# Using the first units' order of work in every unit of a kernel that interleaves a recurrence with a mixture of experts

## The chip, the cores and the metric

One core of one Trainium2 chip. The metric is the device time of one execution in microseconds (us), lower is better. Each run also gives the span of its profile and the mean clock that was granted to TensorE (1 is full). All profiles shown here, and all runs of the variants, were in the fast state. The kernel before varies more (1272 to 1299 us in one set of rounds), and three or four of its runs are marked slow; ratios and gains below use its fast runs alone.

Engines: PE is TensorE's matmuls, PEld its weight loads, DVE VectorE, ACT ScalarE, POOL GpSimd, SP SyncE (here a queue of DMAs). L374 is line 374 of the kernel; in variants with a helper added, lines shift by some ten.

## The reference

Two blocks, one feeding the other. The first is a recurrence over 768 steps for 4 batches of 8 heads with a 40 x 40 state each. The second sends its 3072 x 320 output through four experts (320 to 1024 to 320) and sums them with normalised weights. All is fp32.

```python
for t in range(S):                                   # S = 768
    y[:, :, t] = np.einsum('bhd,bhde->bhe', rt, state)
    Sa = np.einsum('bhde,bhe->bhd', state, at)
    state_decay = state * wt[:, :, None, :] - np.einsum('bhd,bhe->bhde', Sa, bt)
    state = state_decay + np.einsum('bhd,bhe->bhde', vt, kt)
...
for e in range(E):                                   # E = 4
    h = np.maximum(x @ w1[e], 0.0)
    out += p[:, e:e + 1] * (h @ w2[e])
```

## The kernel before

The sequence is cut into 12 chunks of 64 steps, and the batches into two pairs: 24 *units*. For each unit there are three generators of recurrence work, and a list `todo` of mixture pieces (an up-projection `ph`, or half of a down-projection: `p431`, or `p75` and `p26`):

- `within(q)`: work that needs no state. Inputs are transposed on DVE; then come the causal scores `pc` (of V and R) and `pfe`.
- `merge(q)`: three stages, Q's transposes (`Qc`, `QTc`), then `pY`, then `pQ`.
- `step(q)`: `prn`, then `psat`, then `pxr`, `pdy` (the new state and the output Y), then the DMAs from Y into `xT`, the mixture's input.

The parts of `within` that matter: R is the last input to be transposed, and `pc` needs it.

```python
def turn_rv():
    VT = by_channels("VT", "turned", 3, "V")         # a transpose on DVE
    q.RT = by_channels("RT", "RT", 2, "R")           # the next one
    return VT
# ...
NT = by_channels("NT", "turned", 3, "B", rG[:])
q.AT = by_channels("AT", "AT", 2, "A", Gv)
KT = by_channels("KT", "turned", 3, "K", rG[:])
# ...
VT = turn_rv()
yield
pc = quadrants(banks("pc"), 0, BY_TOKENS, L, lambda j, s, i: (
    s, i, j, of_slots(VT, s, j, i, D), of_slots(q.RT, s, j, i, D),
))
```

The mixture's additions run on DVE too: five of `add_h` per expert (`a<-hs`), and eight updates of the output (`osb`). Mixture pieces are taken by `mix`, which after each piece also puts some of the input transfers that are due onto the queue. **How many depends on how many pieces the call takes**:

```python
def begin_later(n):
    for move in later[:n]:
        tc.keep_in_program_order(move(nc.sync))
    del later[:n]

def mix(n):
    for piece in todo[:n]:
        piece()
        begin_later(3 if n > 1 else 6)
    del todo[:n]
```

The loop over units has four gaps for mixture pieces, and two orders of recurrence work around them. The framework's scheduler then orders each engine's instructions; it may move independent ones past each other.

```python
early = u < 5
run(s, 1); run(w, 1); run(s)
# ...
begin_later(len(later))
run(w, 1)                       # rG
if not early: run(m, 1)         # Qc, QTc
gap(1)
# ... the next unit's transfers are listed in `later`
run(w, 1)                       # transposes of B, A, K, V, R
if early: run(m, 1)
else:     run(s_next, 1); run(m, 1)      # prn; pY
gap(2)
if not early: run(m, 1)         # pQ
run(w, 1)                       # pc, pfe
if not early: run(s_next, 1)    # psat
# ...
if early:
    run(m, 1); run(s_next, 1); run(m)    # pY; prn; pQ
    gap(3, 1)                            # one piece
    run(s_next, 1)                       # psat
    mix(0 if 4 * u + 3 in sparse else 1) # one more piece
else:
    gap(3)                               # two pieces at once
```

(The excerpt is shortened, and its comments are mine.)

Of the kernel before, what the change touches and what calls it, by code (L numbers as in the profile page):

```python
# [15 lines left out]
def kernel(  # L16
# [161 lines left out]
    def begin(u):  # L178
        q = Unit()
        q.u, q.c, q.bp = u, u // (B // 2), u % (B // 2)  # L180
        q.b = [2 * q.bp, 2 * q.bp + 1]
        q.start, q.end = q.c == 0, q.c == NC - 1
        q.n = {}
        units.append(q)
        return q

    def load(q, names):
        for x in names:
            q.n[x] = t = sb.tile([P, H, D], FP32, name=f"nat{x}", tag=f"nat{x}", bufs=2 if x == "V" else 1)
            for i, bb in enumerate(q.b):  # L190
                nc.sync.dma_start(
                    out=t[i * L:(i + 1) * L], in_=srcs[x][bb, :, q.c * L:(q.c + 1) * L, :].rearrange("h t e -> t h e"),
                )

    def load_raw(q, names):


        moves = []
        for x in names:
            q.n["raw" + x] = t = raw[x]()  # L200
            heads = srcs[x].rearrange("b h t e -> (b h) t e")[q.b[0] * H:(q.b[1] + 1) * H, q.c * L:(q.c + 1) * L, :]
            heads = heads.rearrange("n (x two) e -> x n (two e)", two=2)
            for r in range(2):
                hs = slice(r, 16, 2)
                for y, los, w_ in ((0, (0,), D + Q), (1, (0, D) if x == "W" else (0,), D - Q if x == "W" else 2 * D - Q)):
                    o = slice(64 * r + Q * y, 64 * r + Q * y + Q)
                    for lo in los:
                        cols = slice(Q * y + lo, Q * y + lo + w_)
                        moves.append(
                            lambda eng, out=t[o, :, lo:lo + w_], in_=heads[:, hs, cols]: eng.dma_start(out=out, in_=in_)  # L210
                        )
        return moves
# [10 lines left out]
    def go(moves, eng=None):  # L223
        for move in moves:
            move(eng or nc.sync)
# [347 lines left out]
    def merge(q):  # L573


        Qc = sb.tile([P, H, Q], FP32, name="Qc", tag="q", bufs=2)
        QTc = sb.tile([P, H, Q], FP32, name="QTc", tag="q", bufs=2)
        tc.keep_in_program_order(nc.vector.transpose(out=dealt(Qc[:]), in_=q.Z))
        tc.keep_in_program_order(
            nc.vector.transpose(  # L580
                out=QTc[:].rearrange("p h r -> p (h r)"), in_=Qc[:].rearrange("p h c -> p (h c)"),
            )
        )
        q.QT = QTs()
        for i in range(P // Q):
            ins = nc.gpsimd.tensor_copy(out=q.QT[quarter(i), :, quarter(i % 2)], in_=QTc[quarter(i)])  # L586
            tc.keep_in_program_order(ins)
        yield

        py = big("pY")  # L590
        for h in range(H):
            for i in (1, 3):
                nc.tensor.matmul(
                    out=py[quarter(i - 1), h * Q:(h + 1) * Q], lhsT=q.F[quarter(i), h, 0:Q],
                    rhs=QTc[quarter(i), h, :], start=True, stop=True,
                )
        Y = sb.tile([P, H, Q], FP32, name="Yq")
        for i in (0, 2):
            nc.scalar.copy(out=Y[quarter(i)].rearrange("p h t -> p (h t)"), in_=py[quarter(i), 0:H * Q])
        yield  # L600

        pq = big("pQ")
        for h in range(H):
            for i in (0, 2):
                nc.tensor.matmul(  # L605
                    out=pq[quarter(i), h * Q:(h + 1) * Q], lhsT=Qc[quarter(i), h, :],
                    rhs=Y[quarter(i), h, :], start=True, stop=True,
                )
        for i in (0, 2):
            nc.scalar.copy(out=q.QT[quarter(i), :, quarter(1)], in_=by(pq[quarter(i), 0:H * Q], Q))  # L610
        yield
# [157 lines left out]
    def mixture_of_unit(q):  # L769

        hs, at = {}, 2 * E * q.u

        def ups(e):
            hs[e] = [up(at + 2 * e + x, q.xT, P, P) for x in range(2)]
            used(at + 2 * e + 2)
            if q.u == 0 and e + 2 < E:
                load_w2(e + 2)

        def down(e):
            po = ps.tile([P, DM], FP32, name="po", tag="mm", bufs=3)  # L780
            for f in range(NF):
                nc.tensor.matmul(  # L782
                    out=po[:], lhsT=hs[e][f // HF][:, f % HF, 0:P], rhs=w2_sb[e][:, f, :],
                    start=(f == 0), stop=(f == NF - 1),
                )
            if e == 0:
                q.osb = outputs()
            add(q.osb[:], po[:], scale(q, e), e == 0)
            if e == E - 1:
                store(q, q.osb)  # L790

        todo.append(lambda: ups(0))
        for e in range(E):
            todo.append(lambda e=e: down(e))
            if e + 1 < E:
                todo.append(lambda e=e: ups(e + 1))
# [113 lines left out]
# [12 lines that stand above are left out]
    def run(gen, n=99):  # L922
        if gen is None:
            return
        for _ in range(n):
            if next(gen, gen) is gen:
                break
# [3 lines left out]
    def begin_step(u):  # L931
        q = units[u]
        if q.bp == 0:
            chunks_x[q.c] = sb.tile([P, 3, 2 * P], FP32, name="xT", tag="xT", bufs=2)
        q.xT = chunks_x[q.c][:, :, q.bp * P:(q.bp + 1) * P]
        return step(q, q.xT)
# [79 lines left out]
    for u in range(1, NU):  # L1016
        q = units[u]
        m = s_next = w = w_next = iter(())
        if u + 1 < NU:
            m, s_next = merge(units[u + 1]), begin_step(u + 1)  # L1020
            w_next = ws[u + 1]
        if u + 2 < NU:
            w = ws[u + 2]

        def gap(n, pieces=None):
            at = 4 * u + n
            run(sum_ops, sums_at.get(at, 0))
            mix((1 if at in sparse else 2) if pieces is None else pieces)

        run(w, 1)  # L1030
        run(w_next)
        run(s, 1)
        gap(0)


        early = u < 5
        run(s, 1)
        run(w, 1)
        run(s)
        if u == 1:  # L1040
            mixture_of_unit(q)
        elif q.bp:
            mixture_of_chunk(units[u - 1:u + 1], chunks_x[q.c])
        begin_later(len(later))
        run(w, 1)
        if not early:
            run(m, 1)
        gap(1)

        if u + 3 < NU:  # L1050
            go(load_raw(begin(u + 3), "W"))
            load(units[u + 3], "BKV")
            later.extend(load_raw(units[u + 3], "BAKVR"))
        run(w, 1)
        if early:
            run(m, 1)
        else:
            run(s_next, 1)
            run(m, 1)
        gap(2)  # L1060

        if not early:
            run(m, 1)
        run(w, 1)
        if not early:
            run(s_next, 1)
        if u + 2 < NU:
            substitute(units[u + 2], nc.gpsimd)
        run(w, 1)
        if u + 3 < NU:  # L1070
            ws.append(within(units[u + 3]))
            run(ws[u + 3], 1)
        if early:
            run(m, 1)
            run(s_next, 1)
            run(m)
            gap(3, 1)
            run(s_next, 1)
            mix(0 if 4 * u + 3 in sparse else 1)
        else:  # L1080
            gap(3)
        s = s_next
# [31 lines left out]
```

## Time and profile before

| | before |
|---|---|
| time, median of 2 fast runs | 1282.74 us (1276.39 to 1289.1) |
| span of the profile, mean granted clock | 1283.8 us, 0.887 |
| the last 16 units but one | 832.8 us, 52.05 us each |
| of these: PE busy, PE idle | 795.45 us, 37.35 us |
| half clock in them | 211.6 us |
| PE's waits for RT in them | 16 of 2.16 us |

The "16 units" are counted from the first `pdy` matmul of one unit to that of the sixteenth unit after it; the same stretch is cut from every trace below. It is the steady part: the start and the tail are not touched by the argument. The table's third and fourth rows come from the view of busy time in a stretch. Its columns are: the stretch, its length, busy us of PE (with the number of instructions), PEld, DVE, ACT and POOL, PE's granted clock, the DMA engines' mean busy share, GB/s.

```profile
312.70:1145.50 832.80, 795.45 (x10529) 696.01 (x10528) 546.04 (x1063) 218.40 (x556) 337.70 (x863) 0.87 0.40 94
```

Idle time is the length less PE's busy time, 37.35 us. A busy PE at clock 0.87 is not a PE at work at full speed: a matmul at half clock counts as busy for longer (16 dense ones took 6.13 us there and 3.72 us at full clock, as the prediction shows). So this line has two kinds of loss in it, idle time and slow busy time, and the count (10529 matmuls) makes the second visible when another kernel does the same matmuls in less busy time.

One more view of before is needed later, the DMA queue's own timeline (start, duration, queue, line, transfer, count):

```profile
629.78 0.97 SPq L210 DMA_DIRECT2D rawR<-in_r_dram  x2
630.85 9.31 SPq L718 DMA_DIRECT2D xT<-Y  x12
640.21 0.97 SPq L210 DMA_DIRECT2D rawR<-in_r_dram  x2
```

Half of R stands behind xT's twelve transfers, and is issued at 640.2 to 641.2 us.

### The profile page before, as it was taken

The page shows a single profiled execution, that of the slowest core. Times are in us where ns is not written, and L with a number is a line of the kernel's source. Part 1 is how long each engine was busy: PE and PEld are TensorE (multiplying, and loading weights), DVE is VectorE, ACT ScalarE, POOL GpSimd, SP SyncE. Part 2 cuts the span into 40 slices and gives each one's busy share as a digit, 9 for nine tenths or more (in the row PEclk, how much of TensorE's full clock was granted, in tenths as well). Part 3 has the DMA queues.
Part 4 walks back from the last instruction along what each step waited for, and adds up shares of the span by engine and source line. Part 5 has one row for each costly group of instructions (what it writes and reads, how often), then busy time and mean ns, then how long its engine had stood idle before and what let it go on. Part 6 is the DMA issues. An engine that isn't in the chain of part 4 may idle for free.

```text
span 1283.8 us, 38036 instructions
## 1 busy us (share of the span) xinstructions
PE 1200.6 (94%) x15828; PEld 1045.6 (81%) x15828; DVE 829.7 (65%) x1642; ACT 331.1 (26%) x844; POOL 475.2 (37%) x1226
## 2 busy tenths in 40 slices
PE   5889988999999999999989999999999999999998
PEld 4767766888788888888878888888888887888887
DVE  7865576789656756676566666676666766644334
ACT  2222333223223122232231322322213323122110
POOL 4024555464253351552524515425244253350000
PEclk7789987999797887997979899789797997899999
DMA  7657642445334424443343443442434334212221
GB/s 147 141 135 196 137 91 67 98 101 125 84 99 100 105 74 99 95 114 85 84 109 85 108 104 87 104 99 72 107 86 112 86 104 89 84 57 86 86 76 31
DMA packets 299491, 126.73 MB, mean 99 GB/s; under 512 B 244360, under 2 KB 272696, under 8 KB 299320
## 3 DMA queue, kind: packets, MB, share of 16 engines
q1 hardware_dynamic: 296312, 123.84, 40.5%
q8 instruction: 125, 2.05, 0.7%
q10 hardware_dynamic: 3008, 0.46, 0.2%
q14 instruction: 46, 0.38, 0.1%
HBM read 116.36 MB, written 3.93 MB: 94 GB/s over the span
## 4 chain that ended last, share of the span: by engine, by line
PE 75%; DVE 10%; SPq 7%; DMA 5%; issue 2%; ACT 1%; DVEq 0%; ACTq 0%
PE ph L741 25%; PE p L848 20%; PE ph L733 9%; SPq L718 3%; PE pfe L374 3%; PE pdy L374 2%; PE psat L374 2%; PE prn L374 2%; DMA w1p<-in_moe_w_dram 2%; PE po L782 2%; SPq L210 2%; PE pxr L374 2%; PE pQ L605 2%; DVE osb L759 2%; PE pc L374 1%
## 5 line engine op out<-in xcount | busy, mean ns | idle before, releaser
L741 PE MATMUL ph<-xT,w1p 128*128 128x256 f32 (+1 forms) x1520 | 370.1, 400 | 0.0
L741 PEld LDWEIGHTS ph<-xT,w1p 128*128 128x128 f32 x1520 | 293.3, 203 | 74.6 <-issue 26.3
L567 POOL TENSOR_TENSOR Z<-Z 128x31 f32<-128x31 f32 (+7 forms) x704 | 256.9, 365 | 55.2
L554 POOL TENSOR_TENSOR Z<-M,Z 128x62 f32<-128x62 f32 (+7 forms) x352 | 156.0, 443 | 294.9 <-DVE M L545 258.6
L842 DVE TENSOR_TENSOR a<-hs 128x512 f32<-128x512 f32 x220 | 152.5, 710 | 145.6 <-ACT hs L746 145.6
L746 ACT ACTIVATE hs<-ph 128x512 f32<-128x512 f32 (+1 forms) x208 | 117.2, 564 | 439.9 <-PE ph L741 439.6
L759 DVE SCALAR_TENSOR_TENSOR osb<-p,gate,osb 128x320 f32<-128x320 f32 (+1 forms) x243 | 108.1, 480 | 128.6 <-PE p L848 125.1
L848 PE MATMUL p<-sums,a 128*128 128x160 f32 x1056 | 164.8, 299 | 0.0
L586 POOL COPY QT<-QTc 32x256 f32<-32x256 f32 x96 | 40.1, 418 | 326.7 <-DVE QTc L580 309.1
L848 PEld LDWEIGHTS p<-sums,a 128*128 128x128 f32 x1056 | 152.9, 190 | 2.2
L733 PE MATMUL ph<-xT,w1p 64*128 64x256 f32 (+1 forms) x760 | 138.1, 442 | 0.6 <-ACT xT L710 0.6
L848 PE MATMUL p<-w,hs 128*128 128x160 f32 x704 | 104.2, 301 | 0.0
L848 PE MATMUL p<-w,a 128*128 128x160 f32 x704 | 102.8, 299 | 0.0
L848 PEld LDWEIGHTS p<-w,hs 128*128 128x128 f32 x704 | 100.8, 191 | 2.3
L848 PEld LDWEIGHTS p<-w,a 128*128 128x128 f32 x704 | 98.0, 190 | 0.0
L733 PEld LDWEIGHTS ph<-xT,w1p 64*128 64x128 f32 x760 | 79.5, 207 | 20.1 <-issue 6.3
L439 DVE RECIPROCAL rG<-G 128x504 f32<-128x504 f32 x24 | 79.1, 3296 | 0.0
L634 ACT COPY SN<-prn 64x256 f32<-64x256 f32 x88 | 32.2, 366 | 159.0 <-DVE EV L630 156.6
L529 DVE STREAM_TRANSPOSE M<-blocks 128x1024 f32<-128x1024 f32 x24 | 46.3, 1931 | 35.4 <-ACT blocks L526 35.1
L374 PE MATMUL pc<-RT,VT 40*64 40x64 f32 x768 | 21.2, 264 | 40.4 <-DVE RT L229 39.0
L374 PEld LDWEIGHTS pc<-RT,VT 40*64 40x64 f32 x768 | 17.3, 168 | 46.7 <-DVE RT L229 43.6
L374 PE MATMUL pdy<-VC,k_tok 64*64 64x104 f32 (+1 forms) x768 | 43.6, 269 | 0.0
(153 smaller groups left out, 1489.7 us busy)
## 6 DMA issues: line engine op xcount, KB each, us to landing
w1p<-in_moe_w_dram SPq DMA_DIRECT2D x95, 512.0 KB
w1p<-in_moe_w_dram SPq DMA_DIRECT2D x190, 64.0 KB
w<-in_moe_w_dram SPq DMA_DIRECT2D x4, 1280.0 KB
sums<-in_moe_w_dram SPq DMA_DIRECT2D x9, 512.0 KB
out_dram<-osb SPq DMA_DIRECT2D x46, 80.0 KB
rawW<-in_w_dram SPq DMA_DIRECT2D x47, 72.0 KB
natB<-in_b_dram SPq DMA_DIRECT2D x42, 80.0 KB
natK<-in_k_dram SPq DMA_DIRECT2D x42, 80.0 KB
```

The source lines that it names most:

```text
L374: nc.tensor.matmul(out=p[row][half(col), lo + at * out_cols:lo + (at + 1) * out_cols], lhsT=lhsT, rhs=rhs, start=(n == 0), stop=(n == len( ...
L439: pin(nc.vector.reciprocal(out=rG[:, :, 0:L - 1], in_=Gv[:, :, 1:L]))
L529: ins = nc.vector.transpose(out=M[:], in_=cols)
L554: ins = eng.tensor_tensor(out=Z[:, 1:3, 0:n, j + 1:Q], in0=M[:, j:j + 2, None, j + 1:Q].to_broadcast([P, 2, n, m]), in1=Z[:, here, 0:n, j: ...
L567: eng.tensor_tensor(out=z[:, 0], in0=z[:, 0], in1=z[:, x], op=ALU.add)
L586: ins = nc.gpsimd.tensor_copy(out=q.QT[quarter(i), :, quarter(i % 2)], in_=QTc[quarter(i)])
L733: nc.tensor.matmul(out=ph[i][:, f, :], lhsT=w1.last[i * DT:(i + 1) * DT, f, :], rhs=xT[i * DT:(i + 1) * DT, 2, :], start=(f == 0), stop=False,
L741: nc.tensor.matmul(out=ph[i][:, f, :], lhsT=w1.main[:, g, at * P:(at + 1) * P], rhs=xT[:, g, :], start=False, stop=(g == 1 and f == HF // ...
L746: nc.scalar.activation(out=h[:, i * HF // 2:(i + 1) * HF // 2, 0:n], in_=ph[i][:], func=ACTF.Relu,)
L759: nc.vector.scalar_tensor_tensor(out=to, in0=p, scalar=sc, in1=to, op0=ALU.mult, op1=ALU.add)
L842: nc.vector.tensor_tensor(out=t[:], in0=x, in1=y, op=op)
L848: nc.tensor.matmul(out=p[:, n * HD:(n + 1) * HD], lhsT=a[:, f, :], rhs=b[:, f, :], start=(f == 0), stop=(f == HF - 1),)
```

## The change

Its intent: the order that the first five units use is used for all.

```diff
-        early = u < 5
+        early = u < 99
```

Three things follow from the one line: `merge`'s and `step`'s small matmuls move to other gaps; the third gap is taken as two calls of one piece instead of one call of two; and so `begin_later` gets six transfers a piece there, not three.

## The prediction

> **What bounds the kernel now.** I began with the page: the engines' busy shares and the slices.

> ```profile
> span 1283.8 us, 38036 instructions
> ...
> PE 1200.6 (94%) x15828; PEld 1045.6 (81%) x15828; DVE 829.7 (65%) x1642; ACT 331.1 (26%) x844; POOL 475.2 (37%) x1226
> ...
> PEclk7789987999797887997979899789797997899999
> ```

> TensorE (PE) is busy 94% of the span, so its idle time alone (some 83 us) seems to leave little. But its granted clock is not full: the slices say 0.7 to 0.9 until the last tenth, and the mean granted clock is 0.887. Two things are therefore to be looked for: where PE waits, and where its clock falls. The waits of PE, longest in total first (columns: total us, times, longest):

> ```profile
> PE pc L374 <- DVE RT L229: 39.0, 18, 3.2
> ...
> PE pY L593 <- DVE QTc L580: 3.5, 4, 1.2
> ...
> PE pQ L605 <- ACT Yq L599: 2.2, 5, 0.7
> PE psat L374 <- DVE EV L630: 1.9, 2, 1.3
> ```

> One wait stands out: the causal scores pc wait for RT, the R input transposed on VectorE (DVE). In the timeline it is the same 2.16 us in each of the 16 units from 334 us to 1115 us. DVE's timeline of one of them says why:

> ```profile
> 637.68 0.70 DVE L229 STREAM_TRANSPOSE VT<-rawV 128x512 f32<-128x512 f32 x1
> 641.51 1.29 DVE L842 TENSOR_TENSOR a<-hs 128x512 f32<-128x512 f32 x2 [3.13 <-ACT hs L746]
> ...
> 646.29 0.38 DVE L759 SCALAR_TENSOR_TENSOR osb<-p,minus_gate,osb 128x160 f32<-128x160 f32 x1
> 646.59 0.70 DVE L229 STREAM_TRANSPOSE RT<-rawR 128x512 f32<-128x512 f32 x1
> ```

> VT is done at 638.4, then DVE sits idle 3.13 us for ACT's hs and works off nine mixture additions; RT stands behind them in DVE's order. PE ran out of mixture work at 645.19.

> The dearer part is what follows. Stretches of PE's busy time and granted clock: three whole units, then the window in which PE waits, the time after it, and the rest of that unit.

> ```profile
> 545.80:593.70 47.90, 45.39 (x660) 40.35 (x660) 34.50 (x68) 13.71 (x35) 21.07 (x53) 0.96 0.43 102
> 593.70:647.35 53.65, 51.49 (x661) 44.89 (x661) 34.49 (x68) 13.71 (x35) 20.85 (x53) 0.84 0.40 94
> 701.90:754.00 52.10, 49.94 (x664) 43.60 (x664) 34.53 (x68) 13.71 (x35) 20.79 (x53) 0.87 0.42 99
> ...
> 590.25:593.66 3.41, 1.30 (x10) 1.06 (x8) 3.28 (x8) 0.00 (x0) 0.00 (x0) 1.00 0.51 67
> 593.66:610.73 17.07, 17.02 (x308) 14.05 (x309) 12.25 (x22) 6.65 (x19) 1.96 (x5) 0.50 0.39 86
> 610.73:644.86 34.13, 34.13 (x353) 30.75 (x352) 19.93 (x42) 7.06 (x16) 18.89 (x48) 1.00 0.39 99
> ```

> In the 3.41 us window with the wait PE is busy 1.30 us. In the next 17.07 us the clock is exactly 0.50, though PE is "busy" 17.02 us. And this stretch is where the old order puts all its small matmuls together (pc, prn, pY, pQ, pfe, psat: nine groups of 32, with hardly anything dense among them)[...]. Half-clock stretches of 3.4, 13.7 or 17.1 us follow each of the 16 waits. Dense work at half and at full clock:

> ```profile
> 605.82 6.13 PE L741 MATMUL ph<-xT,w1p 128*128 128x256 f32 x16
> ...
> 617.76 3.72 PE L741 MATMUL ph<-xT,w1p 128*128 128x256 f32 x16
> ```

> So PE bounds the kernel, and its clock costs more than its waits.

> [...]

> **The change, part by part.** Not one instruction is added or removed; `early` is now true for all units. Before, units from 5 on began the merge of unit u+1 ahead of the second gap and spread its pY and pQ and the next step's prn ahead of and behind the third. Now merge, prn, pQ come behind the third gap, one mixture piece follows, then psat, then one more piece. The built program's order on each engine, compared with the kernel before, repeats every two units and shows:

> 1. DVE: RT directly follows VT, ahead of all the mixture additions, in both kinds of unit (in one ahead of the chunk's first osb updates too, in the other behind four of them). Working from the old durations, with 0 at the end of p431 on PE: four osb updates take 0.25 to 1.9 us, VT and RT 1.4 us, so RT is there at 3.3 us or well before 0. PE now runs 5 or 10 of the 12 matmul pairs of an up-projection before pc, that is 1.6 us (the kind with early RT) or 3.9 us (the other). The data must be there too: the DMA queue used to issue half of R behind xT, until 641.2 for the RT at 646.59; in the new order V and all of R stand ahead of xT, issued by 31.4 us in a unit whose RT comes at 41.7 or later. Wait removed: 2.16 us, 16 times = 35 us.

> 2. PE: the heap of small matmuls is broken up. pc stands inside an up-projection (4.6 us), then come the 4.45 us of p75 and p26, then pfe, pY, prn, pQ (six groups, 3.1 us at the 0.5 us start to start that the full clock shows), an up-projection, psat (1.0), p431 (3.4). With no idle window, no half clock. Its price: the units above took 47.90, 52.10 and 53.65 us at clocks 0.96, 0.87 and 0.84, which is 3.4, 13.7 and 17.1 us at half; (53.65 - 47.90)/(17.1 - 3.4) = 0.42 us lost per half-clock us. A unit with none: 47.90 - 0.42 x 3.4 = 46.5. Less the wait of 2.16 and a pQ wait of 0.36 that this unit has: 44.0. The mean unit is (1115.5 - 334.3)/15 = 52.1, so at most 8.1 us a unit, 16 times: 130 us.

> 3. What takes some back, per unit. pQ waits for ACT's Yq: ACT's new order is F, blocks, Yq; F from 10.3 to 11.0, blocks 0.8, Yq 0.75, ready at 12.6, PE there at 12.2: 0.5. psat needs DVE's EV, in one kind of unit behind the transposes of M and G: ready about 17.9 against 18.3, nearly tight: 0.2 on average. And the clock may fall after all: the cluster from pfe to pQ is of small matmuls with an idle spot. An early unit already runs just that order in the kernel before:

> ```profile
> 122.48 0.69 PE L374 MATMUL pfe<-NT,AT 40*64 40x64 f32 x32
> ...
> 124.69 0.67 PE L374 MATMUL prn<-ident,state 64*64 64x64 f32 x32
> 126.02 0.40 PE L605 MATMUL pQ<-Yq,Qc 32*32 32x32 f32 x13 [0.66 <-ACT Yq L599]
> ```

> No drop followed there; in two of the other three early units a drop followed such a cluster, with longer waits in it. The cluster is 4 us long[...]: I take one unit in four, at 3 us (seven half-clock us x 0.42): 0.75. Sum: 0.5 + 0.2 + 0.75 = 1.45, a unit of 45.4 us, a gain of 6.7 x 16 = 107 us. Prologue (first 280 us) and the tail after 1130 us, which already runs at full clock, stay. 1283 - 107 = 1176; I allow a little for what I can't see and say 1180.

> **Rivals.**
> - *A transfer becomes the bound.* SyncE's queue issues about 36 us of DMAs a unit (xT alone 8.9), in order, and a unit is to shrink to 45. For: w1p is double-buffered and stands behind xT. Against: xT starts at Y, 36.5 us into the unit, ends at 45.4, w1p lands 6 to 7 us later, and that piece is wanted at 58: 6 us of slack; the other three pieces have 8 to 10. PE shows no w1p wait before. If wrong by 3 us a unit: 1225.
> - *The half clock stays.* If six small groups with one idle spot trip it each time for two to four windows, a unit loses 3 to 6 us more: 1210 to 1260. For: two early units. Against: dense work follows at once, and a drop shifts the phase of the next unit.
> - *DVE becomes the bound.* 34.5 us of 45 is 77%, in order. psat waiting for EV, or p75 for the additions, would show as 1 to 2 us a unit: about 1200.
> - *Nothing gained, as the wait only moves*, for instance from RT to QTc (0.9 us in the early units): there QTc was late since gaps held one piece; now QTc is done near 7 us and pY is at 10.6. About 1250.

> **Range and chances.** No drops and no waits gives 1283 - 130 = 1153; the second rival's middle gives some 1230. Faster by over 2% means below 1257, which needs only a fifth of the possible gain: 0.93. Within 2%: 0.05. Slower: 0.02.

> **What would show it right or wrong.** Right: PE's wait for RT gone; the half-clock stretches of the middle fallen from 13 us a unit to a few; mean clock 0.95 or more; units of 44 to 46 us; pc inside an up-projection without idle time; DVE busy unchanged at 830 us. Wrong: waits of PE for w1p, EV, QTc or Yq above 1 us in every unit, or a clock still near 0.89 with half-clock stretches after the cluster from pfe to pQ.

## The result, and the profile after

| | before | after |
|---|---|---|
| time, median of fast runs | 1282.74 us | 1173.5 us (1173.04 to 1173.96, 2 runs) |
| span, mean granted clock | 1283.8 us, 0.887 | 1172.1 us, 0.968 |
| 16 units | 832.8 us | 724.1 us |
| PE busy, idle in them | 795.45, 37.35 us | 704.64, 19.46 us |
| half clock in them | 211.6 us | 6.8 us |

The ratio of the two times is 0.9148 (95% interval 0.8953 to 0.9344): faster. Ratios here are the mean time of one kernel's fast runs over that of the other's of the same rounds, so not quite the ratio of the medians quoted.

The page of after: span, busy shares, and the granted clock in 40 slices.

```profile
span 1172.1 us, 37918 instructions
...
PE 1105.8 (94%) x15828; PEld 964.6 (82%) x15828; DVE 823.0 (70%) x1642; ACT 331.3 (28%) x844; POOL 500.3 (43%) x1226
...
PEclk7798999799999999999999999999999999999999
```

PE's share is 94%, as before, and its instructions are as many; its busy time is 95 us less. The row of the clock tells why: from the ninth slice on it is 9s alone, where before had 7s and 8s. The same stretch of 16 units, then two whole units one after the other, and a clock window around a wait (same view and columns as above; taken in separate questions to the trace):

```profile
310.00:1034.10 724.10, 704.64 (x10529) 618.54 (x10528) 539.88 (x1063) 218.53 (x556) 356.14 (x853) 1.00 0.44 108
...
602.80:648.30 45.50, 43.87 (x661) 38.50 (x660) 35.30 (x68) 13.72 (x35) 22.33 (x55) 1.00 0.46 108
648.30:692.50 44.20, 43.77 (x661) 38.52 (x660) 33.31 (x67) 13.72 (x35) 21.80 (x52) 1.00 0.46 113
...
637.28:640.69 3.41, 2.21 (x42) 1.41 (x42) 2.78 (x6) 0.00 (x0) 0.00 (x0) 1.00 0.11 24
```

The first line gives the account: the same 10529 matmuls take 795.45 - 704.64 = 90.8 us less busy time, and idle time is 37.35 - 19.46 = 17.9 us less; together 108.7 of the 111.7 us between the spans. Five sixths of the gain is clock, one sixth is waiting. The units alternate between 45.5 and 44.2 us, and the last line shows the difference: a wait of 1.20 us, which leaves PE busy for 2.21 of 3.41 us and does not lower the clock.

The waits of PE in after (total us, times, longest):

```profile
PE pc L374 <- DVE RT L229: 14.1, 10, 3.3
...
PE pQ L605 <- ACT Yq L599: 4.8, 15, 0.7
PE prn L374 <- issue: 4.0, 4, 1.2
...
PE pY L593 <- DVE QTc L580: 3.7, 4, 1.2
PE psat L374 <- DVE EV L630: 3.2, 3, 1.6
```

The wait for RT went from 18 times and 39.0 us to 10 times and 14.1 us; it is not gone. It is 1.20 us in every second unit. A wait of 0.28 us for Yq stands now in 12 of the 16 units (before had three, of 0.35 us); new is, in four units, a stop of `prn` that no other engine releases ("issue"). PE's timeline of the unit with the wait, and of `pc` in the next unit (start, duration, operation, output and inputs, shape, count, and in brackets the idle time before it and what ended it):

```profile
637.14 1.14 PE L733 MATMUL ph<-xT,w1p 64*128 64x256 f32 x8
638.21 0.70 PE L741 MATMUL ph<-xT,w1p 128*128 128x256 f32 x2
640.11 0.69 PE L374 MATMUL pc<-RT,VT 40*64 40x64 f32 x32 [1.20 <-DVE RT L229]
640.74 3.29 PE L741 MATMUL ph<-xT,w1p 128*128 128x256 f32 x14
...
651.46 1.07 PE L605 MATMUL pQ<-Yq,Qc 32*32 32x32 f32 x32 [0.28 <-ACT Yq L599]
...
686.49 0.69 PE L374 MATMUL pc<-RT,VT 40*64 40x64 f32 x32
```

`pc` now stands inside an up-projection, with dense matmuls before and behind it. DVE's timeline says which unit waits:

```profile
637.25 1.59 DVE L759 SCALAR_TENSOR_TENSOR osb<-p,gate,osb 128x320 f32<-128x320 f32 x4 [3.24 <-PE p L848]
638.76 0.70 DVE L229 STREAM_TRANSPOSE VT<-rawV 128x512 f32<-128x512 f32 x1
639.39 0.67 DVE L229 STREAM_TRANSPOSE RT<-rawR 128x512 f32<-128x512 f32 x1
...
679.89 0.67 DVE L229 STREAM_TRANSPOSE RT<-rawR 128x512 f32<-128x512 f32 x1
...
682.74 1.01 DVE L757 TENSOR_SCALAR osb<-p,gate 128x320 f32<-128x320 f32 x2 [2.17 <-PE p L848]
```

In one kind of unit VT and RT stand behind the four `osb` updates of p431, though DVE was idle for 3.24 us just before; in the other kind they stand ahead of them and RT is ready 6 us before `pc`. In both, RT comes ahead of all `a<-hs` additions. The DMA queue shows what made that possible:

```profile
621.32 0.89 SPq L210 DMA_DIRECT2D rawR<-in_r_dram  x2
...
624.19 1.08 SPq L210 DMA_DIRECT2D rawR<-in_r_dram  x2
...
630.51 8.90 SPq L718 DMA_DIRECT2D xT<-Y  x12
```

All of R is now ahead of xT.

### The profile page after: what moved, and what is told of

Same layout as the page of the kernel before. It is cut to its first block, busy times and chain, and to the rows that moved or that the text cites. A ratio compares the mean times of both kernels' runs of the same rounds, so it can differ in the third digit from the quotient of the medians.

```text
span 1172.1 us, 37918 instructions
## 1 busy us (share of the span) xinstructions
PE 1105.8 (94%) x15828; PEld 964.6 (82%) x15828; DVE 823.0 (70%) x1642; ACT 331.3 (28%) x844; POOL 500.3 (43%) x1226
## 4 chain that ended last, share of the span: by engine, by line
PE 84%; DVE 7%; ACT 3%; issue 2%; DMA 2%; SPq 1%; DVEq 0%; ACTq 0%
PE ph L741 30%; PE p L848 28%; PE ph L733 8%; PE pdy L374 3%; PE po L782 3%; PE psat L374 2%; PE pxr L374 2%; PE pfe L374 2%; PE pQ L605 1%; PE pc L374 1%; PE pev L374 1%; ACT blocks L526 1%; DVE osb L759 1%; DVE M L529 1%; PE pg L341 1%
## 5 line engine op out<-in xcount | busy, mean ns | idle before, releaser
L741 PE MATMUL ph<-xT,w1p 128*128 128x256 f32 (+1 forms) x1520 | 351.7, 383 | 0.0
L741 PEld LDWEIGHTS ph<-xT,w1p 128*128 128x128 f32 x1520 | 275.7, 192 | 64.0 <-issue 20.5
L567 POOL TENSOR_TENSOR Z<-Z 128x31 f32<-128x31 f32 (+7 forms) x704 | 273.0, 388 | 55.2
L746 ACT ACTIVATE hs<-ph 128x512 f32<-128x512 f32 (+1 forms) x208 | 117.3, 564 | 437.1 <-PE ph L741 436.7
L842 DVE TENSOR_TENSOR a<-hs 128x512 f32<-128x512 f32 x220 | 155.4, 723 | 108.9 <-ACT hs L746 108.9
L759 DVE SCALAR_TENSOR_TENSOR osb<-p,gate,osb 128x320 f32<-128x320 f32 (+1 forms) x243 | 107.9, 481 | 103.6 <-PE p L848 99.1
L586 POOL COPY QT<-QTc 32x256 f32<-32x256 f32 x96 | 48.7, 507 | 287.4 <-DVE QTc L580 283.6
L733 PE MATMUL ph<-xT,w1p 64*128 64x256 f32 (+1 forms) x760 | 106.9, 399 | 0.6 <-ACT xT L710 0.6
L733 PEld LDWEIGHTS ph<-xT,w1p 64*128 64x128 f32 x760 | 65.7, 189 | 16.5 <-issue 6.5
L381 DVE COPY_PREDICATED VC<-mask_up,pc 128x256 f32<-128x256 int32 x48 | 18.5, 440 | 39.8 <-PE pc L374 39.8
L495 ACT ACTIVATE F<-pfe 128x256 f32<-128x256 f32 x48 | 15.8, 381 | 100.6 <-PE pfe L374 100.6
L374 PE MATMUL pdy<-VC,k_tok 64*64 64x104 f32 (+1 forms) x768 | 43.5, 269 | 0.0
```

Source lines behind the costliest of these rows:

```text
L374: nc.tensor.matmul(out=p[row][half(col), lo + at * out_cols:lo + (at + 1) * out_cols], lhsT=lhsT, rhs=rhs, start=(n == 0), stop=(n == len( ...
L567: eng.tensor_tensor(out=z[:, 0], in0=z[:, 0], in1=z[:, x], op=ALU.add)
L586: ins = nc.gpsimd.tensor_copy(out=q.QT[quarter(i), :, quarter(i % 2)], in_=QTc[quarter(i)])
L733: nc.tensor.matmul(out=ph[i][:, f, :], lhsT=w1.last[i * DT:(i + 1) * DT, f, :], rhs=xT[i * DT:(i + 1) * DT, 2, :], start=(f == 0), stop=False,
L741: nc.tensor.matmul(out=ph[i][:, f, :], lhsT=w1.main[:, g, at * P:(at + 1) * P], rhs=xT[:, g, :], start=False, stop=(g == 1 and f == HF // ...
L746: nc.scalar.activation(out=h[:, i * HF // 2:(i + 1) * HF // 2, 0:n], in_=ph[i][:], func=ACTF.Relu,)
```

## The experiments

Two causes are bound together in the one line: the order of the matmuls, and the pace of the transfers. And two losses are bound together in before: the wait of 2.16 us, and the half clock behind it, in a heap of small matmuls. The experiments take these apart; the last ones try what is left. Ratios are against before in the same rounds, fast runs with fast runs, and each result was correct. The mean of before's fast runs was 1279.9 us for experiments 1 to 4, 1285.7 us for the forced `pc`, 1281.2 us for experiments 6 to 9 and 1282.9 us for the last two; gains are counted from these. The record's verdict is "faster" for experiments 5 to 11 and "unclear" for 1 to 4, where before has only four fast runs of seven. The intervals of 1, 3 and 4 lie below 0.98 all the same; that of 2 reaches 0.9842. From each variant one execution was traced.

### 1. The old order with a faster pace of transfers

```diff
 # in before
-            begin_later(3 if n > 1 else 6)
+            begin_later(6)
```

> Old order of work, but six transfers of the next unit's inputs begun with each mixture piece instead of three, so that all of R is issued ahead of xT. In the built program RT then stands right behind VT and pc right behind p431, and the heap of small matmuls is cut in two. Theory A (the gain of the change came from RT's transfer and so RT's place in VectorE's order): most of the gain appears without the change of order, 1180 to 1220 us; in every second unit RT stands behind four additions and pc waits some 3.3 us there, 8 times, each with a short half-clock stretch. Theory B (the new order of merge, pY, prn, pQ and psat itself made the gain): within 2% of the kernel before, 1260 to 1290 us.

Measured: 1222.39 us (1219.64 to 1226.16), ratio 0.9553 (0.9475 to 0.963), clock 0.936. PE's timeline where `pc` is released:

```profile
564.46 0.83 PE L374 MATMUL pc<-RT,VT 40*64 40x64 f32 x32 [2.30 <-DVE RT L229]
...
567.49 1.06 PE L593 MATMUL pY<-QTc,F 32*32 32x32 f32 x32 [0.50 <-DVE QTc L580]
```

So 57 us (64.7 us in the 16 units of the traces), somewhat over half of the gain, come without any change of the order written in the loop: only transfers are issued earlier. The edit goes further than the change, which issues six a piece in the third gap alone; here all gaps do, and all of R is issued some 12 us ahead of xT. R's position in the queue moves, the scheduler puts RT right behind VT or behind the four `osb` updates, and `pc` right behind p431. Waiting does not get less (it is 45.9 us in the 16 units, more than before's 37.35: 2.30 us for RT in every second unit, and waits of 0.2 to 3.2 us for QTc); the half clock falls from 211.6 to 78.5 us. `pY` and `pQ` with `pfe` now lie apart, with dense pieces between them; that this is why was not tested alone. The time is just outside theory A's 1180 to 1220 us, and the wait 2.30 us where 3.3 was expected.

Not each of the eight waits of 2.30 us brought half clock: two did not. Both lay across the end of a clock window. Here is one of the two, in three windows (columns as for the stretches above):

```profile
851.61:855.02 3.41, 1.75 (x13) 1.50 (x12) 1.62 (x5) 0.00 (x0) 2.63 (x9) 1.00 0.07 18
855.02:858.44 3.42, 2.61 (x132) 2.44 (x134) 2.76 (x7) 0.22 (x1) 1.79 (x7) 1.00 0.40 112
858.44:861.85 3.41, 3.41 (x21) 2.75 (x18) 0.00 (x0) 2.57 (x7) 1.10 (x3) 1.00 0.59 148
```

So where a wait of 2.30 us happens to fall seems to count: these two windows hold 1.75 and 2.61 us of busy time, while the falls behind the waits of 2.16 us in before (16 of 16) and of 2.30 us in experiment 5 (8 of 8) came at 1.10 to 1.33 us, once at 1.86. No sharp limit comes out of these runs: 1.75 us did not bring half clock here, and 1.86 us did there.

### 2. The new order with the old pace of transfers

```diff
 # in after
-            begin_later(3 if n > 1 else 6)
+            begin_later(3 if n > 1 or units[-1].u > 7 else 6)
```

> New order of work, but only three transfers begun with each mixture piece, as in the kernel before; half of R is again issued behind xT, and the built program again has RT behind the additions and pc behind p26. Theory A: the wait of about 2.2 us for RT is back in 16 units, with half-clock stretches behind it of 7 to 14 us since seven groups of small matmuls follow: 1240 to 1285 us. Theory B: the gain stays, 1175 to 1200 us.

Measured: 1249.21 us (1247.57 to 1253.41), ratio 0.9765 (0.9689 to 0.9842), clock 0.912.

```profile
586.27 0.69 PE L374 MATMUL pc<-RT,VT 40*64 40x64 f32 x32 [2.16 <-DVE RT L229]
586.79 0.65 PE L374 MATMUL pfe<-NT,AT 40*64 40x64 f32 x32
587.25 0.65 PE L374 MATMUL pfe<-AT,KT 40*64 40x64 f32 x32
588.83 1.06 PE L593 MATMUL pY<-QTc,F 32*32 32x32 f32 x32 [0.93 <-DVE QTc L580]
```

The order alone gives 30 us (31.9 us in the 16 units). The old wait of 2.16 us is back in all 16 units, and the half clock follows each of them, for 6.8 or 10.2 us instead of mostly 13.7 or 17.1. The two halves sum to 57 + 30 = 87 us, of the 106 us that after gained (experiment 6); in the 16 units to 97 of 109. Each gain is uncertain by some 10 us and the first edit goes further than the change, so whether the two simply add is not shown. The new order by itself does *not* bring RT forward; the pace of the transfers does.

### 3. The wait filled with idle work, in the old order

```diff
 # in before, behind gap(2)
+        if not early and u < 22:
+            dummy = ps.tile([P, P], FP32, name="dummy", tag="mm", bufs=3)
+            for _ in range(9):      # two instructions each in the profile
+                tc.keep_in_program_order(nc.tensor.matmul(out=dummy[:], lhsT=ident[:], rhs=ident[:], start=True, stop=True))
```

> Kernel before, with nine matmuls of the identity (a result that nobody reads, about 2.2 us) put on TensorE between p26 and pc, where it otherwise stands idle. RT comes no earlier. If the idle window is what halves the clock: the wait's 35 us stay (as filler), the half-clock stretches of the middle fall from 212 us to under 40, gain 0.42 x 180 = 75 us: 1195 to 1215 us. If the heap of small matmuls behind it halves the clock by itself: the stretches stay, 1265 to 1290 us.

Measured: 1238.96 us (1237.98 to 1242.15), ratio 0.9689 (0.9598 to 0.978), clock 0.946.

```profile
577.73 2.17 PE L1065 MATMUL dummy<-ident 128*128 128x128 f32 x18
580.05 0.69 PE L374 MATMUL pc<-RT,VT 40*64 40x64 f32 x32
...
584.03 0.24 PE L605 MATMUL pQ<-Yq,Qc 32*32 32x32 f32 x2 [0.67 <-ACT Yq L599]
...
586.66 1.05 PE L374 MATMUL psat<-QT,EV 64*64 64x64 f32 x28
```

The filler takes just the time of the wait (2.17 us), so no time is won from the wait itself. Yet the kernel is 40 us faster (48.6 us in the 16 units), because the half clock fell from 211.6 to 58.0 us. So in these units idle time in the window was the main trigger: 153.6 of the 211.6 us went with it. A long wait is not needed: the heap with its wait of 0.67 us still set the half clock off in six units; three more stretches follow stops of "issue" kind ahead of `psat`, of 1.31 to 3.48 us. I had expected 1195 to 1215 us. In the 16 units the gain was to be 75 us; the missing 26 us are the half clock that stayed (some 11 us at 0.42), the wait for Yq that slow matmuls had covered (10.8 us, before 1.1) and the stops (8.0 us, before 1.8).

### 4. RT first in the old order

```diff
 # in before; behind(ins, other) adds a dependency without a semaphore, so the scheduler orders ins after other
+                if x == "R":
+                    rt[:] = [ins]                   # RT's transpose
...
+                if rt: behind(ins, rt[0])           # each a<-hs addition of add_h
...
+                if rt: behind(ins, rt[0])           # the first osb updates of down_2
```

> Kernel before, with RT alone moved ahead of the mixture additions in VectorE's order by a dependency; TensorE's order and the heap stay, and half of R is still issued behind xT, landing about 2 us before pc wants RT. If the wait and the half clock both hang on RT: the wait falls below 0.5 us, the half-clock stretches below 60 us, 1160 to 1190 us, as fast as the changed kernel. If the heap matters by itself: wait gone, stretches stay, about 1245 us.

Measured: 1221.99 us (1218.66 to 1226.34), ratio 0.955 (0.9473 to 0.9627), clock 0.931. `pc` no longer waits, but a new wait appears inside the heap:

```profile
577.15 0.92 PE L382 MATMUL pfe<-NT,AT 40*64 40x64 f32 x24 [1.33 <-ACT SN L645]
```

The half clock follows each of these, for 6.8 or 3.4 us, 95.6 us in all. A wait of 1.33 us here sets it off 16 times; the waits of 1.20 us in after, with dense matmuls around them, never did. In 12 of the 16 the window before the fall held less than 1.20 us of idle time (0.88 to 1.15), while in after and its repeat 11 waits of 1.20 us lay whole in one window; so it is not the difference of 0.13 us that counts. In these traces, then, what lay around a wait counted, not its length alone. The result fell between the two expectations.

### 5. `pc` forced ahead of the up-projection, in the new order

```diff
 # in after
+            pc_last[:] = last_mm                    # the last matmul of pc
...
+                if pc_last and n == 2 * P:
+                    behind(ins, pc_last[0])         # the first matmuls of the up-projection
```

> Changed kernel, with pc forced ahead of the whole up-projection that otherwise covers it. In every second unit RT is not yet there (behind four additions that follow p431), so TensorE stands idle some 3.3 us, but with only one group of small matmuls (0.5 us) and then 9 us of dense work behind it: a wait without a heap. If the wait sets off the half clock and the heap sets how long it lasts: a half-clock stretch of 3.4 or at most 6.8 us after each of the 8 waits, 8 x (2.1 more wait + 0.42 x 4) = 30 us more: 1195 to 1212 us. If the wait alone brings stretches as long as in the kernel before (14 to 17 us): 1225 us or more. If a wait in dense surroundings brings none: about 1190 us.

Measured: 1210.61 us (1209.22 to 1214.34), ratio 0.9428 (0.9357 to 0.9498), clock 0.95.

```profile
565.53 0.69 PE L382 MATMUL pc<-RT,VT 40*64 40x64 f32 x32 [2.30 <-DVE RT L237]
566.16 2.00 PE L742 MATMUL ph<-xT,w1p 64*128 64x256 f32 x8
568.09 4.28 PE L753 MATMUL ph<-xT,w1p 128*128 128x256 f32 x15
```

The clock windows around it (same columns as the stretches above):

```profile
562.92:566.33 3.41, 1.11 (x37) 0.80 (x37) 2.26 (x6) 0.00 (x0) 0.00 (x0) 0.99 0.08 18
566.33:569.74 3.41, 3.41 (x12) 2.33 (x13) 1.67 (x4) 0.00 (x0) 1.41 (x4) 0.51 0.60 167
569.74:573.15 3.41, 3.41 (x19) 3.07 (x19) 0.00 (x0) 1.13 (x2) 0.55 (x2) 1.00 0.50 93
```

All eight waits of 2.30 us are followed by half clock; with dense matmuls right behind, it lasts a single window of 3.4 us (6.8 us after the first). In before, with the heap behind, it lasted 13.7 or 17.1 us in 13 of 16 units, and 3.4 us in the other three; what spared these was not found. The last window of the 13 longer stretches held 3.41 us of dense matmuls (128 columns), that of the three short ones 3.41 us of small ones, so that only dense work ends half clock is not shown. Here, then, the wait set the fall off (8 of 8), and where the heap followed, half clock mostly lasted longer (13 of 16). (Three more stretches here, 13.7 us in all, follow stops of "issue" kind.) This also shows what the scheduler's placing of `pc` inside the up-projection is worth: some 36 us against after in its own rounds, 26 of them in the 16 units.

### 6. After once more

> The changed kernel once more, so that the three below are compared with it in the same rounds: 1171 to 1176 us.

Measured: 1174.81 us (1170.2 to 1179.3, 6 runs), ratio 0.9177 (0.9116 to 0.9238). The result holds. In this trace there is no half clock at all in the 16 units, with the same waits; the two single windows in the first trace of after each follow a stop of "issue" kind (1.25 us ahead of `prn`, 0.55 us ahead of `pQ`), and these change from one execution to the next.

### 7 to 9. What is left in after: the wait for RT, the wait for Yq, both

```diff
 # RT ahead: in after, down_1
+                if rt: behind(ins, rt[0])           # p431's first osb updates
 # pY early: in after
-        if not early:
-            run(m, 1)
+        run(m, 1)                                   # pY ahead of pfe
...
-            run(m, 1)
             run(s_next, 1)
```

> Changed kernel, with RT put ahead of the first additions of p431 in VectorE's order in both kinds of unit (in the changed kernel it stands behind four of them in every second unit, and pc waits 1.20 us there, 8 times after 360 us). If that order is what is left of the wait: pc's waits in the middle gone, 8 x 1.2 = 9.6 us less, 1160 to 1167 us. If R's data or the additions' delay are in the way, or the clock drops more often at another phase: unchanged, 1170 to 1178 us.

> Changed kernel, with pY ahead of pfe, so that ScalarE's copies Yq come ahead of its copies of F and pQ no longer waits 0.28 us in some 13 units. Theory: that idle spot goes, 4 us less, and no window of the cluster trips the clock (two drops before): 1166 to 1171 us. Rival: pY now waits for QTc, or F and M come later and psat waits for EV: 1173 to 1180 us.

> Both of the above: if they add up, 1173 - 9.6 - 4 = 1160 us (1156 to 1164), units of 44 us, clock 0.97 or more over the whole; if one undoes the other, 1165 to 1172 us.

Measured: RT ahead 1171.25 us (1167.32 to 1174.95), ratio 0.9142 (0.9081 to 0.9203); pY early 1176.3 us (1174.66 to 1178.21), ratio 0.9182 (0.9133 to 0.9232); both 1166.52 us (1161.84 to 1170.99), ratio 0.9105 (0.9052 to 0.9158). Each did in the steady part what it should: with RT ahead the waits for RT are gone and units take 44.2 us; with pY early the waits of 0.28 us are gone. But the gain was lost at the start, in whole or in part: all three fell in the second range that was expected, and the first two do not differ from after by more than its runs do among themselves. `pc` of unit 7 begins at 277.5 us in after, at 288.9, 286.1 and 291.4 us in these three. With RT ahead, `pc` of unit 6 waits 3.99 us for RT, as R's data comes late and the additions that are tied to RT wait too, and 13.7 us of half clock follow. With pY early nothing is tied to RT; there `pY` waits 1.86 us for QTc near 248 us, and 10.2 us of half clock follow.

### 10 and 11. The same for the later units only

```diff
-                if x == "R":
+                if x == "R" and q.u > 7:            # both kernels
...
+        if u > 5:                                   # the second one: pY early
+            run(m, 1)
...
+            if u <= 5:
+                run(m, 1)
```

> RT ahead of p431's additions as before, but from unit 8 on alone. In the run of all units the middle gained (units of 44.2 us against 44.9, no wait for RT) but the start lost some 11 us: the pc of unit 7 came at 288.9 us instead of 277.7, with a half-clock stretch of 13.7 us at 244 us that the changed kernel does not have. If the start lost because of the edit there, the start is as in the changed kernel and the gain of the middle shows whole: 1161 to 1167 us. If the start varies by itself from build to build: 1168 to 1175 us.

> RT ahead (from unit 8 on) and pY ahead of pfe (from step 6 on). In the run of both for all units the middle ran at 43.3 to 45 us a unit, but the pc of unit 7 came 13.7 us late. If that was the edit's doing in the early units: 1166.5 - 13 = 1153 us (1150 to 1158). If not: 1163 to 1169 us.

Measured: RT ahead 1162.55 us (1160.31 to 1168.19), ratio 0.9061 (0.9022 to 0.9099); both **1155.8 us** (1150.45 to 1158.5), ratio 0.9006 (0.8969 to 0.9043). Both times are as expected; the second is the fastest kernel of the study, 1.6% below after (in other rounds). In the second, `pc` of unit 7 begins at 279.5 us, and most units have no wait left. In the trace of the first (its slowest run, 1168.19 us) that `pc` begins at 283.8 us though nothing is edited so early: a few us of the start change by themselves. PE's timeline, then DVE's:

```profile
633.16 0.70 PE L752 MATMUL ph<-xT,w1p 128*128 128x256 f32 x2
633.79 0.69 PE L382 MATMUL pc<-RT,VT 40*64 40x64 f32 x32
634.42 3.29 PE L752 MATMUL ph<-xT,w1p 128*128 128x256 f32 x14
...
644.63 0.69 PE L616 MATMUL pQ<-Yq,Qc 32*32 32x32 f32 x32
```

```profile
629.56 0.67 DVE L237 STREAM_TRANSPOSE RT<-rawR 128x512 f32<-128x512 f32 x1
632.21 1.59 DVE L769 SCALAR_TENSOR_TENSOR osb<-p,gate,osb 128x320 f32<-128x320 f32 x4 [1.98 <-PE p L858]
```

RT runs in the idle time of DVE that after left unused, and neither `pc` nor `pQ` has a bracket. What idle time PE still has is eight stops of "issue" kind.

### All runs side by side

The 16 units of each trace, read as for before; matmuls are as many in each (but for the filler's).

| kernel | 16 units, us | PE busy | PE idle | half clock |
|---|---|---|---|---|
| before | 832.8 | 795.5 | 37.4 | 211.6 |
| new order, old pace | 800.9 | 754.0 | 46.9 | 146.8 |
| filler | 784.2 | 763.0 | 21.2 | 58.0 |
| old order, faster pace | 768.1 | 722.2 | 45.9 | 78.5 |
| RT first, old order | 764.7 | 739.4 | 25.3 | 95.6 |
| `pc` forced | 750.3 | 719.3 | 31.0 | 44.4 |
| after | 724.1 | 704.6 | 19.5 | 6.8 |
| fastest | 706.8 | 698.2 | 8.6 | 6.8 |

Take 44.0 us a unit (the prediction's), the idle time, and 0.42 us per half-clock us (the prediction's too): before gives 16 x 44.0 + 37.4 + 0.42 x 211.6 = 830 against 832.8; after 726 against 724.1; RT first 769 against 764.7; `pc` forced 754 against 750.3; the filler, with 16 x 2.17 = 34.7 us added for itself, 784 against 784.2. Three come out too high: the faster pace in the old order (783 against 768.1), the old pace in the new order (812 against 800.9) and the fastest (715 against 706.8). In the first two, waits for QTc lie inside the half-clock stretches; if a slow clock does not lengthen a wait, 0.42 charges too much there, but no run isolates this. All three kernels with pY early come out 8 to 9 us too high, as if their unit without any loss were 0.5 us shorter; why is open.

## Why the prediction was right

The time was 1173.5 us against 1180 predicted, within 1150 to 1230, and faster as given with 0.93. By its own steps:

**What bounds the kernel.** Right. PE bounds it, and the clock costs more than the waits: 90.8 us of busy time against 17.9 us of idle time. That the idle window trips the clock and that the heap draws the half clock out was read from one trace; the filler (211.6 to 58.0 us of half clock) and the forced `pc` (3.4 us behind seven of eight waits, against 13.7 or 17.1 us behind 13 of 16) agree with both.

**Part 1, the wait for RT.** Half right. RT did come ahead of all `a<-hs` additions in both kinds of unit, but the wait was not removed 16 times: 1.20 us remained in every second unit, 0.6 us on average. The step that failed is the pairing "1.6 us (the kind with early RT) or 3.9 us (the other)". It is the other way round: the unit whose RT stands behind four `osb` updates is the one where PE has 5 pairs of matmuls before `pc`, as the two timelines of after show (8 + 2 matmuls, then the wait). With the right pairing the prediction's own numbers give it: RT at 3.3 us on its scale and PE there after 1.6 us leave 1.7 us of waiting; measured, 1.20 us. The prediction also saw that R would stand ahead of xT, but credited all to the order of work; experiments 1 and 2 show that the pace of transfers is what moves R, and that a faster pace is worth 57 us by itself and the order 30.

**Part 2, the heap.** Right. The heap is broken up, `pc` runs inside an up-projection, and the half clock in the 16 units fell from 211.6 to 6.8 us. 0.42 us per half-clock us holds for most of the runs (measured against the matmuls' busy time of after it is at most 0.46: filler, (763.0 - 34.7 - 701.8) / 58.0, where 701.8 is after's busy time less its own 0.42 x 6.8; and as little as 0.26: old order, faster pace, (722.2 - 701.8) / 78.5; the low end is rough, as busy time without any half clock differs by some 6 us between kernels), and the unit of 44.0 us without any loss stands (44.2 us in after with 0.43 us idle; 43.3 us in the fastest kernel).

**Part 3, what takes some back.** Right in the sum, by luck in the terms. Predicted were 0.5 us for Yq, 0.2 for EV and 0.75 for falls of the clock, 1.45 together. Measured per unit: Yq 0.28 us in 12 of the 16, so 0.21; EV nothing; falls of the clock 0.42 x 6.8 / 16 = 0.18 (and none in the second trace); the wait for RT 0.6, which was not in the list; stops of "issue" kind some 0.3, which were not either. That is 1.3 us, and a mean unit of 724.1 / 16 = 45.3 us against 45.4 predicted. The three listed terms were 1.1 us too large together, and the two that were not listed come to 0.9. The most mis-sized term is the falls of the clock: one unit in four at 3 us was predicted, the author's estimate, and two units in 16 with a single window each came.

**The rivals.** None came true. No wait of PE's matmuls for w1p shows (its weight loads have eight, of at most 0.3 us), so transfers are not the bound. The half clock does not stay. DVE is busy 823.0 us in all, as little as before, and EV holds nothing up in the steady part. The wait did move in part, but to 1.20 us and not to QTc; QTc does return as a wait where the transfers keep their old pace (0.93 us, experiment 2).

**What it said would show it.** PE's wait for RT gone: no, 1.20 us in every second unit. Half clock from 13 us a unit to a few: 0.4 us. Clock 0.95 or more: 0.968. Units of 44 to 46 us: 44.2 and 45.5. `pc` inside an up-projection: yes, but "without idle time" only in every second unit. DVE unchanged: 823.0 against 829.7 us.

**The stops of "issue" kind** are all of the idle time over 0.15 us that the fastest kernel still has in its 16 units. The traces say what they coincide with. Here is the stop of 1.25 us in after, and of the DMA queues between 557.8 and 558.9 us the one whose kind the profile gives as "instruction" (packets, MB, share):

```profile
560.20 0.33 PE L374 MATMUL prn<-ident,state 64*64 64x64 f32 x4 [1.25 <-issue]
...
q8 instruction: 1, 0.02, 5.5%
```

In the 16 units of all 13 traces there are 69 such stops, of 0.15 to 3.48 us; each of the 69 ended 1.26 to 1.64 us after a packet of 16 KB on this queue had landed, which only 7 of PE's 201 other waits did. There is one such packet to some 254 of PE's matmuls and weight loads. My reading of these times is that PE had run out of instructions there; the small matmuls use them up fastest (32 of them with their weight loads in some 0.5 us, against 16 dense ones in 3.72 us). No run moves the packets, so it was not tested. RT first and the new order with the old pace have no such stop.

## What to carry to other kernels

When PE's busy share is high and its granted clock is not full (94% and 0.887 in before), look at each stretch of half clock and at the window just before it: a short wait there can cost several times its own length (in before 2.16 us, and some 7 us more behind it, 0.42 x 17.1, where 17.1 us at half clock followed). Give small matmuls dense neighbours: waits of 1.20 or 1.21 us with dense matmuls around them brought half clock in none of 18 cases (two traces of after), while waits of about 1.33 us in the heap brought it in each of 16 units (RT first); and with dense matmuls right behind a wait of 2.30 us it ended after 3.4 us in seven of eight cases (`pc` forced). And when a change of order moves the time, ask what else the same line moves; here the queue's pace, hidden in an argument of `mix`, was about half of the effect.
